# Moving the last subtraction of layer 1's softplus from VectorE to GpSimd

## The chip, the cores and the metric

One core of one Trainium2 chip. The metric is the device time of one execution in microseconds, the median over runs. The engines are named as in the profile: PE (TensorE; PEld is its weight load), DVE (VectorE), ACT (ScalarE), POOL (GpSimd), SP (SyncE, which issues most DMAs).

## The reference, cut to what matters

Three blocks follow one another over 2 x 576 = 1152 tokens with 512 features: an attention with a learned bias, a dense block (layer 1 and layer 2), and a routed block with one of 8 experts per token. The change lies in the dense block:

```python
def _moe_ref(x, w_in, w_out):                # x 1152 x 512, w_in 512 x 2048, w_out 2048 x 512
    h = x @ w_in                                             # layer 1
    g = np.maximum(h, 0.0) + np.log1p(np.exp(-np.abs(h)))    # softplus
    return (g @ w_out).astype(np.float32)                    # layer 2
```

## The kernel before, in words

The kernel runs in stages: attention (to about 175 us), layer 1 (175 to 277), layer 2 for the first six token tiles (to about 342), then layer 2 for the last three token tiles mixed with the routing, and the experts.

*Layer 1.* The 2048 hidden features are cut into 16 slices f of 128 (the loop at L627). The attention output lies transposed in SBUF, split into a high and a low part (x0hi, x0lo), and each weight slice likewise (whi, wlo). For a slice PE makes 3 x 12 matmuls at L640: three groups of 384 tokens, four chunks of 128 input features, and three products (high with high, high with low, low with high). The result ph takes three PSUM banks; two ph buffers take turns, so the matmuls of slice f+2 need that everything that reads ph of slice f is done.

*Softplus of a slice.* ACT computes ea = |h| (L653), ea = exp(-ea) (L654), la = ln(1 + ea) (L655) and ua = ea + 1 (L656), each over 128x1152. DVE then computes gA = max(h, 0) + la for the first 768 tokens (L657) and gB for the last 384 (L659); these two and L653 are the readers of ph. The rounding error that lies in 1 + ea is taken out afterwards: ua = (ua - 1) - ea (L661), then gA = gA - ua (L663) and gB = gB - ua (L664). Tiles ua, la and ea have two buffers each. gA and gB keep all 16 slices: gA is what layer 2 reads for token tiles 0 to 5, gB for the last three token tiles (it lies in the tiles gBt).

*Beside it on DVE and ACT.* The weights come as 64-bit floats and are converted and split on chip: L128 on ACT, L129, L130, L131 and L133 on DVE, then L149 (ACT) and L150 (DVE) for the slices of w_in, L619 (ACT) and L620 (DVE) for those of w_out. During layer 1 this is done for the w_in slices ahead and for the first four w_out slices.

*Layer 2.* g is split into a high and a low part again: L681 on ACT and L682 on DVE, from gA and, for the last three token tiles, from gB; the matmuls are L673 to L675.

*Order.* In the attention stage the order on each engine is the order written (a manual schedule). There GpSimd has work beside DVE: L316 scales the softmax rows, while DVE makes, among others, the hidden values of the bias (L219). In layers 1 and 2 no order is written by hand: the compiler's scheduler orders the instructions of each engine from dependences, the order of the program and its own costs, and sets the semaphores. In layer 1 no instruction runs on GpSimd; later ones are memsets and the indirect DMAs of the experts.

Of the kernel before, what the change touches and what calls it, by code (L numbers as in the profile page):

```python
# [17 lines left out]
ALU = mybir.AluOpType  # L18
# [59 lines left out]
def build(ctx: ExitStack, tc: tile.TileContext, I, out, dbg=None):  # L78
    nc = tc.nc
# [56 lines left out]
    def win_tiles(pool, f):  # L136
        return tuple(pool.tile([P, 4, P], F32R, tag=k, name=f"{k}{f}", bufs=NW1) for k in ("whi", "wlo"))
# [14 lines left out]
    def win_load(pool, f, whi, wlo):  # L152
        yield from win_split(pool, f, win_raw(pool, f), whi, wlo)

    def run(gen):
        for _ in gen:
            pass
# [4 lines left out]
    with ExitStack() as ac:  # L162
# [261 lines left out]
        with tc.manual_schedule(engines=order | {nc.sync.engine}):  # L424
# [60 lines left out]
            for n in range(N + DEPTH + 2):  # L485
# [13 lines left out]
                if n == 8:  # L499
                    nc.vector.tensor_reduce(out=sel4, in_=ident.rearrange("p (c e) -> p e c", c=4), axis=AX.X,  # L500
                                            op=ALU.add)
# [89 lines left out]
    with ExitStack() as mc:  # L591
# [20 lines left out]
        gB = [gBt[0][:, f] if f < 4 else gBt[1][:, f - 4] for f in range(16)]  # L612

        def wout_load(f):
            raw = wp2.tile([P, DM, 2], U32, tag="raw", name=f"raw_out{f}")
            nc.sync.dma_start(raw.rearrange("p f w -> p (f w)"), I["moe_w_out"].bitcast(U32)[P * f:P * f + P, :])
            w32 = wp2.tile([P, DM], F32, tag="w32", name=f"wout{f}", bufs=1)
            run(f64_to_f32(wp2, raw, w32, f"cout{f}"))
            nc.scalar.copy(wohi[f], w32)  # L619
            nc.vector.tensor_tensor(out=wolo[f], in0=w32, in1=wohi[f].bitcast(F32), op=ALU.subtract)  # L620

        with ExitStack() as c1:
            c1.push(x0c)
            c1.push(wc)
            sp = c1.enter_context(tc.tile_pool(name="sp", bufs=2, side="right", reuse_waits="tile"))
            ps_h = c1.enter_context(tc.tile_pool(name="ps_h", bufs=2, space=PSUM, reuse_waits="tile"))
            for f in range(16):  # L627
                if f >= 16 - 2 * NW0 and f % 2 == 0:
                    wout_load((f - 16 + 2 * NW0) // 2)
                whi, wlo = win_ready.pop(0)  # L630
                if f + NW1 < 16:
                    win_ready.append(win_tiles(wp, f + NW1))
                    run(win_load(wp, f + NW1, *win_ready[-1]))
                ph = ps_h.tile([P, 3, 512], F32, tag="ph", name=f"ph{f}")
                for n in range(3):
                    xk, o = (0, 384 * n) if n < 2 else (1, 0)
                    k = 0
                    for c in range(4):
                        for ws, xs in ((whi, x0hi), (whi, x0lo), (wlo, x0hi)):
                            nc.tensor.matmul(ph[:, n, :384], ws[:, c, :], xs[xk][:, c, o:o + 384],  # L640
                                             start=(k == 0), stop=(k == 11))
                            k += 1
                if f == 14:
                    for k, (ghi, glo) in enumerate(g0):
                        g = gA[k].rearrange("p a n -> p (a n)")[:, :2 * P]
                        nc.scalar.copy(ghi, g)
                        nc.vector.tensor_tensor(out=glo, in0=g, in1=ghi.bitcast(F32), op=ALU.subtract)
                hv = ph[:, :, :384]
                ua = sp.tile([P, 3, 384], F32, tag="ua", name=f"ua{f}")
                la = sp.tile([P, 3, 384], F32, tag="la", name=f"la{f}")  # L650
                ea = sp.tile([P, 3, 384], F32, tag="ea", name=f"ea{f}")

                nc.scalar.activation(ea, hv, AF.Abs)  # L653
                nc.scalar.activation(ea, ea, AF.Exp, scale=-1.0)  # L654
                nc.scalar.activation(la, ea, AF.Ln, bias=1.0)  # L655
                nc.scalar.activation(ua, ea, AF.Copy, bias=1.0)  # L656
                nc.vector.scalar_tensor_tensor(out=gA[f], in0=hv[:, 0:2], scalar=0.0, in1=la[:, 0:2],  # L657
                                               op0=ALU.max, op1=ALU.add)
                nc.vector.scalar_tensor_tensor(out=gB[f], in0=hv[:, 2], scalar=0.0, in1=la[:, 2],  # L659
                                               op0=ALU.max, op1=ALU.add)  # L660
                nc.vector.scalar_tensor_tensor(out=ua, in0=ua, scalar=1.0, in1=ea,  # L661
                                               op0=ALU.subtract, op1=ALU.subtract)
                nc.vector.tensor_tensor(out=gA[f], in0=gA[f], in1=ua[:, 0:2], op=ALU.subtract)  # L663
                nc.vector.tensor_tensor(out=gB[f], in0=gB[f], in1=ua[:, 2], op=ALU.subtract)  # L664


        c2 = ExitStack()
# [589 lines left out]
```

## Time and profile before

| what | us |
|---|---|
| median of 3 runs | 439.5 (438.65 to 441.52) |
| the profiled execution | 438.52 |
| its span, first to last instruction | 436.7 |

The profile is of one execution. In rows of instructions the first number is the start in us from the span's start, the second the duration in us, then engine, line, operation, output and inputs, shapes and count; in square brackets stands how long the engine sat idle before and what ended that. DVE starts an instruction shortly before the one ahead has ended, so durations in a row overlap a little. PEclk is the granted TensorE clock as a share of 2.4 GHz.

### The profile page before, as it was taken

To read this page: it belongs to the slowest core of one execution; us is meant where nothing else is said; L and a number is where in the kernel's file an instruction comes from. 1 tells how busy PE (TensorE), PEld (TensorE's weight loads), DVE (VectorE), ACT (ScalarE), POOL (GpSimd) and SP (SyncE) were. 2 spreads that over 40 slices of the span, in tenths; PEclk is the share of its full clock that TensorE was granted. 3 is DMA by queue.
4 is the path that set the end of the run, shared out by engine and by line. 5 is a ranking of instruction groups with operands and counts; after the bars stand their busy time and mean duration, and the time that the engine had idled before them with its cause. 6 is when DMAs were issued, how large, how long until landed. Compare 5 with 4: busy or idle time off the path is not lost.

```text
span 436.7 us, 8984 instructions
## 1 busy us (share of the span) xinstructions
PE 416.5 (95%) x3355; PEld 325.6 (75%) x3355; DVE 334.0 (76%) x869; ACT 276.5 (63%) x520; POOL 71.1 (16%) x97
## 2 busy tenths in 40 slices
PE   8989999999999998999999999999999998999994
PEld 6225667676677666999999999878888776877741
DVE  5799788889989877799999999999993425625501
ACT  5788888888899896698987878844551332121010
POOL 3014342333455541000000000000000000201001
PEclk9999999999999999999999999999999999999998
DMA  6799974766874413431323101133430700799600
GB/s 167 208 267 374 350 247 139 223 176 175 228 244 171 173 50 114 169 105 49 103 91 95 50 2 48 23 124 96 146 97 0 288 2 2 262 366 404 252 2 23
DMA packets 38579, 66.60 MB, mean 153 GB/s; under 512 B 4288, under 2 KB 17860, under 8 KB 38528
## 3 DMA queue, kind: packets, MB, share of 16 engines
q1 hardware_dynamic: 37520, 64.38, 45.9%
q10 hardware_dynamic: 592, 0.80, 0.5%
q0 software_dynamic: 416, 0.77, 0.5%
q8 instruction: 28, 0.46, 0.4%
q14 instruction: 23, 0.19, 0.1%
HBM read 49.80 MB, written 16.69 MB: 152 GB/s over the span
## 4 chain that ended last, share of the span: by engine, by line
PE 57%; DVE 10%; ACT 4%; issue 1%; DMA 1%; POOL 0%; POOLq 0%; DVEq 0%; ACTq 0%
PE ph L640 17%; PE px L673 5%; PE px L674 5%; PE px L675 5%; PE po L369 4%; PE sc L297 2%; PE bhA L980 2%; PE bhB L980 2%; PE byB L988 2%; PE pt L327 1%; DMA xbJ<-out_dram,tiJ 1%; DVE hid L219 1%; DVE ua L661 1%; PE sc_None L297 1%; DVE ep L303 1%
## 5 line engine op out<-in xcount | busy, mean ns | idle before, releaser
L316 POOL TENSOR_SCALAR ep<-ep,st 128x576 f32<-128x576 f32 x62 | 51.7, 846 | 93.5 <-DVE st L314 64.1
L640 PE MATMUL ph<-x0hi,whi 128*128 128x384 f32 x192 | 64.5, 336 | 0.6 <-DVE gBt L659 0.6
L640 PE MATMUL ph<-x0hi,wlo 128*128 128x384 f32 x192 | 64.2, 334 | 0.0
L640 PE MATMUL ph<-x0lo,whi 128*128 128x384 f32 x192 | 64.2, 334 | 0.0
L219 DVE TENSOR_SCALAR hid<-U 128x320 f32<-128x320 f32 (+17 forms) x134 | 56.4, 480 | 2.4 <-PE pb L224 2.3
L297 PE MATMUL sc<-kst,qr 64*128 64x288 f32 x256 | 50.9, 431 | 2.3 <-DVE st L303 1.9
L309 ACT ACTIVATE ep<-ep,st 128x576 f32<-128x576 f32 x64 | 49.0, 772 | 0.0
L297 PEld LDWEIGHTS sc<-kst,qr 64*128 64x128 f32 x256 | 28.8, 185 | 25.5 <-issue 12.5
L303 DVE CUSTOM_DVE_ANT_0 ep<-sc,bias 128x576 f32<-128x576 f32 x64 | 45.6, 750 | 2.8 <-PE sc L297 1.7
L232 ACT ACTIVATE bsb<-pb,isc 128x287 f32<-128x287 f32 (+31 forms) x72 | 31.7, 493 | 17.1 <-PE pb L224 15.8
L224 PE MATMUL pb<-hid,pw 128*32 128x512 f32 (+18 forms) x320 | 37.7, 486 | 2.0 <-ACT bsb L232 1.9
L369 PE MATMUL po<-at,vn 128*64 128x128 f32 (+1 forms) x512 | 38.4, 292 | 0.3 <-DVE x0lo L387 0.3
L640 PEld LDWEIGHTS ph<-x0hi,whi 128*128 128x128 f32 x192 | 36.0, 188 | 1.9 <-issue 1.6
L640 PEld LDWEIGHTS ph<-x0lo,whi 128*128 128x128 f32 x192 | 36.0, 188 | 0.0
L640 PEld LDWEIGHTS ph<-x0hi,wlo 128*128 128x128 f32 x192 | 36.0, 188 | 0.0
L347 ACT COPY at<-pt 128x512 f32<-128x512 f32 x64 | 34.1, 586 | 1.8 <-PE sc L327 0.7
L369 PEld LDWEIGHTS po<-at,vn 128*64 128x64 f32 x512 | 29.1, 136 | 4.2 <-DVE x0lo L387 0.5
L327 PEld LDWEIGHTS pt<-ident,ep 64*128 64x128 f32 x512 | 26.9, 138 | 5.5 <-issue 1.2
L327 PE MATMUL pt<-ident,ep 64*128 64x64 f32 x512 | 29.6, 226 | 0.9 <-ACT at L347 0.9
L681 ACT CAST ghiB<-gBt 128x384 fp32r<-128x384 f32 x16 | 8.2, 513 | 29.6 <-PE px L674 29.6
L682 DVE TENSOR_TENSOR gloB<-gBt,ghiB 128x384 fp32r<-128x384 f32 x16 | 8.9, 556 | 21.2 <-ACT ghiB L681 16.0
L673 PE MATMUL px<-wohi,ghiA 128*128 128x512 f32 x64 | 25.0, 390 | 0.0
(416 smaller groups left out, 860.7 us busy)
## 6 DMA issues: line engine op xcount, KB each, us to landing
biasd<-bsb SPq DMA_DIRECT2D x40, 295.5 KB, 3.6
bias<-biasd SPq DMA_DIRECT2D x19, 576.0 KB, 5.4
raw_in<-in_moe_w_in_dram SPq DMA_DIRECT2D x16, 512.0 KB, 3.8
raw_out<-in_moe_w_out_dram SPq DMA_DIRECT2D x16, 512.0 KB, 3.4
ex<-in_moe_w_dram SPq DMA_DIRECT2D x8, 1024.0 KB, 15.5
ew<-in_moe_w_dram SPq DMA_DIRECT2D x4, 1024.0 KB, 4.8
qr<-in_p_q_dram SPq DMA_DIRECT2D x10, 256.0 KB, 4.8
kst<-in_p_k_dram SPq DMA_DIRECT2D x8, 288.0 KB, 6.7
```

Of the source, the lines that this page charges most:

```text
L219: nc.vector.tensor_scalar(self.hid[c][:, :self.R], U[:, :self.R], Lt[:, g:g + 1], 0.0, ALU.add, ALU.max)
L224: nc.tensor.matmul(ps[32 * c:32 * c + 32, :hi - lo], w2b, self.hid[c][:, lo:hi], start=True, stop=True, tile_position=(0, 32 * c))
L232: nc.scalar.mul(dst, src, isc[:, s:s + 1])
L297: nc.tensor.matmul(self.sc[j][qs_, c, :288], self.q[js, self.hp, b, qs_], kst[js, self.hp, b, 288 * c:288 * c + 288], start=True, stop=Tru ...
L303: nc.vector.tensor_tensor_reduce(out=self.ep[:, j].rearrange("p (c k) -> p c k", c=2), in0=self.sc[j][:, :, :288], in1=bias.rearrange("p ( ...
L309: nc.scalar.activation(self.ep[:, j], self.ep[:, j], AF.Exp, bias=self.st[:, j, 0:1], scale=-1.0, accum_out=self.st[:, j, 1:2])
L316: eng.tensor_scalar(self.ep[:, j], self.ep[:, j], self.st[:, j, 3:4], 0.0, ALU.mult, ALU.add)
L327: nc.tensor.matmul(self.pt[:, r, c] if c < 8 else p5[r], flat[rs_, o:o + P], ident[rs_, rs_], is_transpose=True, start=True, stop=True, ti ...
L347: nc.scalar.copy(at.rearrange("p j c n -> p (j c) n")[:, :, off:off + 64], self.pt[:, r])
L369: nc.tensor.matmul(po[64 * j:64 * j + 64, :n], vn[:, self.hp, c, self.b, j, :], at[:, j, c, :n], start=(c == 0), stop=False, tile_position ...
L640: nc.tensor.matmul(ph[:, n, :384], ws[:, c, :], xs[xk][:, c, o:o + 384], start=(k == 0), stop=(k == 11))
L673: nc.tensor.matmul(px, ghi[:, cs], wohi[f], start=(f == 0), stop=False)
```

## The change

The subtraction at L664, one per slice and 16 in all, is issued on GpSimd instead of VectorE. Operands, tiles and all other lines stay.

```diff
                 nc.vector.tensor_tensor(out=gA[f], in0=gA[f], in1=ua[:, 0:2], op=ALU.subtract)
-                nc.vector.tensor_tensor(out=gB[f], in0=gB[f], in1=ua[:, 2], op=ALU.subtract)
+                nc.gpsimd.tensor_tensor(out=gB[f], in0=gB[f], in1=ua[:, 2], op=ALU.subtract)
```

## Rows read from the trace of the kernel before

**Rows 1.** The page's first part: busy time and share of the span.

```profile
PE 416.5 (95%) x3355; PEld 325.6 (75%) x3355; DVE 334.0 (76%) x869; ACT 276.5 (63%) x520; POOL 71.1 (16%) x97
```

**Rows 2.** Busy time of each engine in layer 1.

```profile
core 0: us, PE busy (x) PEld busy (x) DVE busy (x) ACT busy (x) POOL busy (x), PEclk, DMA share, GB/s
174.70:276.80 102.10, 101.45 (x583) 100.47 (x582) 98.43 (x154) 86.39 (x100) 0.00 (x0) 1.00 0.24 76
```

**Rows 3.** PE's waits, 174.7 to 342: us in total, times, longest.

```profile
PE ph L640 <- DVE gBt L659: 0.6, 1, 0.6
PE px0pl L675 <- DVE gloA L682: 0.3, 1, 0.3
```

**Rows 4.** PE in order of time: first matmuls of blocks and of layer 2.

```profile
174.71 0.44 PE L640 MATMUL ph<-x0hi,whi 128*128 128x384 f32 x1
...
187.30 0.36 PE L640 MATMUL ph<-x0hi,whi 128*128 128x384 f32 x1
...
206.32 0.33 PE L640 MATMUL ph<-x0hi,whi 128*128 128x384 f32 x1
...
212.56 0.35 PE L640 MATMUL ph<-x0hi,whi 128*128 128x384 f32 x1
...
251.74 0.41 PE L640 MATMUL ph<-x0hi,whi 128*128 128x384 f32 x1 [0.65 <-DVE gBt L659]
...
276.78 0.39 PE L675 MATMUL px0pl<-wohi,glo 128*128 128x512 f32 x1
```

**Rows 5.** DVE in order of time, slice 0 of layer 1.

```profile
186.56 0.55 DVE L659 SCALAR_TENSOR_TENSOR gBt<-ph,la 128x384 f32<-128x384 f32 x1
187.02 1.35 DVE L661 SCALAR_TENSOR_TENSOR ua<-ua,ea 128x1152 f32<-128x1152 f32 x1
188.29 0.68 DVE L150 TENSOR_TENSOR wlo<-win,whi 128x512 fp32r<-128x512 f32 x1
...
189.76 0.55 DVE L664 TENSOR_TENSOR gBt<-gBt,ua 128x384 f32<-128x384 f32 x1
190.23 0.68 DVE L133 SCALAR_TENSOR_TENSOR win<-raw_in,cin6a 128x512 uint32<-128x512 uint32 x1
```

**Rows 6.** The tile gBt: durations in ns (min/median/max), first and last start.

```profile
L664 DVE TENSOR_TENSOR gBt<-gBt,ua x16: 549/552/554, 189.8 to 285.3; 128x384 f32<-128x384 f32 x16
L681 ACT CAST ghiB<-gBt x16: 512/513/515, 329.9 to 376.5; 128x384 fp32r<-128x384 f32 x16
```

**Rows 7.** POOL's groups by line: busy us, mean ns, idle before.

```profile
L316 POOL TENSOR_SCALAR ep<-ep,st 128x576 f32<-128x576 f32 x62 | 51.7, 846 | 93.5 <-DVE st L314 64.1 <-DVE x0lo L387 12.9 <-ACT at L347 6.8
...
L190 POOL MEMSET v<- 128x1024 f32 x1 | 0.9, 941 | 0.0
L921 POOL MEMSET xbB<- 128x512 f32 x1 | 0.5, 545 | 0.0
```

**Rows 8.** DVE beside POOL in order of time, around 125 and 141 us.

```profile
124.93 1.12 DVE L133 SCALAR_TENSOR_TENSOR win<-raw_in,cin0a 128x512 uint32<-128x512 uint32 x1
...
124.76 0.75 POOL L316 TENSOR_SCALAR ep<-ep,st 128x576 f32<-128x576 f32 x1 [1.41 <-ACT x0hi L383]
...
140.99 0.69 DVE L150 TENSOR_TENSOR wlo<-win,whi 128x512 fp32r<-128x512 f32 x1
...
141.14 1.17 POOL L316 TENSOR_SCALAR ep_None<-ep_None,st_None 128x576 f32<-128x576 f32 x1 [1.48 <-ACT whi L149]
```

**Rows 9.** DVE, then POOL, in order of time around 108 us.

```profile
107.67 0.50 DVE L219 TENSOR_SCALAR hid<-U 128x560 f32<-128x560 f32 x1
...
108.51 0.92 DVE L219 TENSOR_SCALAR hid<-U 128x560 f32<-128x560 f32 x1
109.35 0.99 DVE L219 TENSOR_SCALAR hid<-U 128x560 f32<-128x560 f32 x1
...
107.76 1.36 POOL L316 TENSOR_SCALAR ep<-ep,st 128x576 f32<-128x576 f32 x1 [2.79 <-DVE x0lo L387]
109.10 0.93 POOL L316 TENSOR_SCALAR ep<-ep,st 128x576 f32<-128x576 f32 x1
```

## The prediction

> **What bounds the kernel now.** I read the page first, then the table of the two stretches around the change, then who waited for whom, then the instructions in order of time. The page shows TensorE (PE) busy for 95% of the 436.7 us span and VectorE (DVE) for 76% [rows 1]. That share hides the stage that matters. In layer 1 (174.7 to 276.8 us) DVE is busy 98.4 us of 102.1 while GpSimd (POOL) is not busy at all, and the TensorE clock is granted at its upper level (1.00, 2.4 GHz) [rows 2]. The reader is to see two engines loaded to the brim beside an idle one.
>
> Which of the two sets the pace? The list of waits names only one wait of PE on DVE in layer 1, 0.6 us, and one of 0.3 us early in layer 2 [rows 3]. The starts of the blocks say a little more. An undisturbed slice f of layer 1 (36 matmuls) takes from 206.32 to 212.56, that is 6.24 us; 16 of them are 99.8 us. Layer 1 takes from 174.71 to 276.78, that is 102.1 us [rows 4]. So some 2.2 us go to PE standing still or starting late, 0.65 of it the labelled wait at 251.74 [rows 4]. The reason is the pair of ph buffers: slice f+2 can't start before L657 and L659 of slice f have read theirs. L659 of slice 0 ends at 186.56 + 0.55 = 187.11 and PE starts slice 2 at 187.30, 0.19 us later [rows 4, 5]. PE is thus the bound, with DVE about a tenth of a microsecond behind it: DVE work taken away can give back 2.2 us of layer 1 at most, DVE work added comes out as time almost at once.
>
> **The change part by part.**
>
> *Removed from DVE:* 16 subtractions L664 of 128x384, 552 ns each [rows 6]. DVE overlaps the end of one instruction with the start of the next, so the place in the queue that one gives back is start to start: 189.76 to 190.23, 0.47 us [rows 5]. 16 x 0.47 = 7.5 us of DVE, all inside layer 1 but the last two slices, whose L659 PE doesn't wait for in layer 1; 14 x 0.47 = 6.6 us bear on PE.
>
> *Added to GpSimd:* 16 subtractions with two inputs from SBUF. The trace has none. Nearest rows: two memsets, 128x1024 in 941 ns and 128x512 in 545, so 0.77 ns per element and 0.15 us fixed; and the tensor_scalar of 128x576, 846 ns in the mean [rows 7], 0.75 us where nothing delays it [rows 8]. (0.75 - 0.15) / 576 = 1.04 ns per element read. If two inputs are streamed side by side, 384 x 1.04 + 0.15 = 0.55 us; if one after the other, 768 x 1.04 + 0.15 = 0.95 us; if the fixed part and a slower loop both come on top, twice the whole tensor_scalar, 1.5 us. I take 0.95, the one between. POOL is idle in layer 1 [rows 2], so the 16 never queue behind one another at a period of 6.2 us, and no DMA is issued behind them there; the memset of a later stage is all that follows.
>
> *Nobody is late for the result itself:* gB is first read by the cast L681 at 329.9, 44 us after the last L664 at 285.3 [rows 6]. The ua buffer (two deep) is now released by POOL, and is written again by L656 two slices, about 12 us, later; POOL's finish about 1.6 us (one DVE instruction of delay and 0.95) after L661 is far inside that. The rooms of layer 1's tiles that layer 2 takes over are released by the last POOL instruction instead of the last L664, at most about 1 us later; that bounds a cost from above, and I take nothing, because PE's only wait early in layer 2 is one of 0.3 us for something else [rows 3], taken up below.
>
> *What does cost: DVE and POOL delay each other.* The attention stage shows it. Four equal DVE instructions L219 follow one another; the first starts at 107.67 and lasts 0.50, the third and fourth start at 108.51 and 109.35 and last 0.92 and 0.99 [rows 9]. The two that lengthen stand beside the two POOL instructions that start at 107.76 and 109.10. POOL's first takes 1.36 us instead of 0.75: it waits for DVE, then DVE waits for it. Together DVE loses 0.42 + 0.49 = 0.91 us to 2 x 0.75 = 1.5 us of POOL work. An instruction with two inputs suffers too: L133 takes 1.12 us beside a POOL instruction [rows 8] and 0.68 alone [rows 5], a loss of 0.44. And POOL waits behind a two-input DVE instruction, 1.17 us behind L150 [rows 8]. So one POOL instruction of 0.75 us costs DVE about 0.45 us, 0.30 less than its own time, or six tenths of it.
>
> In layer 1 POOL's subtraction becomes ready when L661 ends. DVE then has the next instruction, a split of weights or L663, started without a gap (L150 at 188.29 in slice 0 [rows 5]); POOL gets in behind it and the DVE instruction after that waits. With 0.95 us the loss is 0.57 (six tenths) to 0.65 (0.30 less); I take 0.60. DVE's balance per slice is -0.47 + 0.60 = +0.13 us, and over 14 slices +1.8 us. Some of it falls into the 3.7 us that DVE still idles in layer 1 [rows 2], mostly in the first slices, and a POOL instruction that meets L657 or L659 may cost nothing; I leave 0.8 off and keep +1.0 us. The balance is small because the change swaps a DVE instruction for a wait of DVE of about the same length.
>
> The Trainium skill, "GPSIMD Engine Reference", section "3. Performance versus the Vector engine", puts a two-input elementwise instruction on GpSimd at 1.96 times VectorE's time. On L664 that would be an estimate of 1.08 us, a loss of about 0.7 and some +3 us over the 14 slices; no run here shows the ratio.
>
> *After layer 1* PE's only wait on DVE, 0.3 us [rows 3], is for a gloA; even if all of it went, 0.3 us would be won, and I count none; the rest of the kernel shifts with the end of layer 1.
>
> *Sum.* The profiled execution took 438.5 us (span 436.7 and 1.8 around it). 438.5 + 1.0 = 439.5 in its terms. The median of the runs shown is 439.5, 1.0 above this execution, so the forecast in the median's terms is **440.5 us**: no change that can be told (about 1%, 4.4 us, is what a measurement of this kernel can tell from none).
>
> **The rivals.**
>
> *A. DVE wins.* If POOL streams both inputs together (0.55 us) the loss is 0.25 to 0.33 and DVE's balance -0.14 to -0.22 per slice; if POOL mostly meets L657 and L659, it is the full -0.47. PE's 2.2 us of late starts [rows 4] then shrink, half to all of them: 439.5 - 2.2 = 437.3 at best, some 438.3 in the middle. For it: POOL is idle, and 0.13 us per slice is little to be wrong by. Against it: POOL becomes ready in the middle of DVE's two-input work, not beside L657. Faster by over 1% isn't in it, since layer 1 has only 2.2 us to give.
>
> *B. The exchange makes DVE the bound of layer 1 (slower).* Its place is the DVE instruction behind POOL's in every slice; its price is POOL's whole time instead of six tenths. With 0.95 us blocked in full DVE's balance is +0.48 per slice, 14 x 0.48 = 6.7 us, 446.2; with 0.55 it is +0.08, or 1.1 us. It decides from a loss of 0.47 us up: beyond that every tenth of a microsecond is 1.4 us of kernel. For it: DVE idles only 3.7 us of 102 [rows 2] and PE starts within 0.2 us of the release [rows 4, 5]. Against it: the four rows of L219 show a loss smaller than POOL's time [rows 9]. The Trainium skill, "SBUF — State Buffer", section "Who interferes with whom", speaks for this one: a VectorE instruction with two SBUF inputs and a GpSimd instruction that reads SBUF exclude each other, and the second blocks in full until the first is done. That L133 and L150's neighbour both stretch agrees with the exclusion [rows 8]; that the loss is only six tenths doesn't agree with a price of the whole time.
>
> *C. Another order.* Outside the attention stage the compiler's scheduler orders each engine's instructions from its own costs; with 16 fewer on DVE it may pull weight splits ahead of L657 or behind it. The shown order already costs 2.2 us, so the swing is of that size: 437.5 to 442.5.
>
> **How the numbers follow.** Forecast 0.48 (own range 439 to 442), A 0.22, B 0.18, C 0.12. The range that leaves two in ten out goes from A's best, 437.3, to the middle of B, 444.5. Faster by over 1%: below 435.1, only an order of C much better than the present one, 0.03. Slower by over 1%: above 443.9, two thirds of B and a little of C, 0.14. Same: 0.83.
>
> **What would show it.** In the profile after: L664 on POOL x16 near 0.95 us without a wait and up to 1.5 with one; DVE instructions that follow L661 lengthened by about 0.6 us, L657 and L659 not; DVE's busy time in layer 1 about as before although 8.8 us of instructions left it; layer 1 between 102 and 104 us. A step is wrong if the L664 on POOL lasts over 1.2 us (then B), if DVE rows stay at their old lengths (then A), or if layer 1 is longer with DVE idle in it (then C). The forecast fails if layer 1 changes by more than 4 us.

## The result and the profile after

| | before | after |
|---|---|---|
| median of 4 runs each, us | 439.07 (438.30 to 441.52) | 444.06 (442.85 to 445.45) |
| ratio of after to before | | 1.009, 95% interval 1.0061 to 1.0120 |
| the profiled execution and its span, us | 438.52, 436.7 | 442.85, 441.1 |

The change makes the kernel slower, by 5.0 us in the medians and 4.3 in the two profiled executions. The page of after, first part and the new group of POOL (busy us, mean ns, idle before); it answers to [rows 1, 6]:

```profile
PE 417.5 (95%) x3355; PEld 325.7 (74%) x3355; DVE 336.1 (76%) x853; ACT 277.6 (63%) x520; POOL 105.9 (24%) x113
...
L664 POOL TENSOR_TENSOR gBt<-gBt,ua 128x384 f32<-128x384 f32 x16 | 35.0, 2189 | 87.7 <-DVE ua L661 65.8
```

DVE has 16 instructions fewer and is busy 2 us longer. POOL's subtractions take 2.19 us in the mean, their waiting included, where 0.95 was forecast. The stretch of layer 1 in after, which answers to [rows 2], and PE's waits (us in total, times, longest), which answer to [rows 3]:

```profile
174.64:280.47 105.83, 102.74 (x582) 100.43 (x581) 101.62 (x145) 88.14 (x101) 31.83 (x14) 1.00 0.25 79
```

```profile
PE ph L640 <- DVE gBt L659: 1.1, 3, 0.5
PE px0pl L675 <- DVE gloA L682: 1.0, 1, 1.0
PE ph L640 <- ACT whi L149: 1.0, 2, 0.6
PE ph L640 <- ACT ea L653: 1.0, 1, 1.0
```

Layer 1, from its first matmul to the first of layer 2, takes 105.83 us instead of 102.07, that is 3.76 more; the wait for gloA early in layer 2 grows from 0.3 to 1.0 us. Together they are the span's 4.4 us within a tenth: the time was lost in layer 1 and in this one wait behind it.

What happens there is plain in the order of time. DVE and POOL of after in two slices; of slice 1 only the instructions from L150 to L659 of the next slice:

```profile
188.23 0.69 DVE L150 TENSOR_TENSOR wlo<-win,whi 128x512 fp32r<-128x512 f32 x1
188.45 1.34 POOL L664 TENSOR_TENSOR gBt<-gBt,ua 128x384 f32<-128x384 f32 x1 [21.93 <-issue]
188.83 1.77 DVE L663 TENSOR_TENSOR gA<-gA,ua 128x768 f32<-128x768 f32 x1
...
195.67 0.68 DVE L150 TENSOR_TENSOR wlo<-win,whi 128x512 fp32r<-128x512 f32 x1
195.82 4.15 POOL L664 TENSOR_TENSOR gBt<-gBt,ua 128x384 f32<-128x384 f32 x1 [6.04 <-DVE ua L661]
196.27 0.95 DVE L663 TENSOR_TENSOR gA<-gA,ua 128x768 f32<-128x768 f32 x1
...
198.68 0.41 DVE L130 TENSOR_SCALAR cin8a<-cin8m 128x512 uint32<-128x512 uint32 x1
199.01 0.95 DVE L657 SCALAR_TENSOR_TENSOR gA<-ph,la 128x768 f32<-128x768 f32 x1
199.88 0.54 DVE L659 SCALAR_TENSOR_TENSOR gBt<-ph,la 128x384 f32<-128x384 f32 x1
```

In slice 0 POOL waits for L150, then runs, and L663 waits for POOL: 1.77 us instead of 0.95. In slice 1 POOL starts about as soon after L150's start (0.15 us, 0.22 in slice 0), but DVE keeps the turn: L663 and four more follow undisturbed, and POOL ends only at 199.97, after DVE has come to L657. L657 and L659 are not lengthened. The tile ua over all slices of after (ns: min/median/max), and the three lengthened DVE instructions that are not L663:

```profile
L663 DVE TENSOR_TENSOR gA<-gA,ua x16: 946/1768/1779, 188.8 to 287.4; 128x768 f32<-128x768 f32 x16
L664 POOL TENSOR_TENSOR gBt<-gBt,ua x16: 1132/1416/4414, 188.4 to 287.5; 128x384 f32<-128x384 f32 x16
```

```profile
236.82 0.85 DVE L129 TENSOR_SCALAR cin13m<-cin13m 128x512 f32<-128x512 f32 x1 [0.31 <-ACT cin13m L128]
...
264.37 1.40 DVE L131 SCALAR_TENSOR_TENSOR cout4a<-raw_out,cout4a 128x512 uint32<-128x512 uint32 x1
...
288.30 1.51 DVE L620 TENSOR_TENSOR wolo<-wout,wohi 128x512 fp32r<-128x512 f32 x1
```

L663 is lengthened by 0.82 us in nine slices, 7.4 us in all; with these three (0.43, 0.72, 0.83) DVE loses 9.4 us in 12 slices. In the other four (1, 3, 4 and 6) it loses nothing. That is against the 7.5 us that it was relieved of. Two of the twelve blocks, those of the last two slices (L663 at 281.21 and L620 at 288.30), lie behind layer 1; inside it ten blocks take 7.7 us, against 14 subtractions or 6.6 us of relief. L129 reads a single input: an instruction with one input can be blocked too.

But the scheduler also gave DVE, ACT and PE another order of instructions. So two theories stood. Theory 1: DVE and POOL exclude each other, and the blocks cost the time. Theory 2: the new order costs it.

### The profile page after: what moved, and what is told of

Same layout as the page of the kernel before. It is cut to its first block, busy times and chain, and to the rows that moved or that the text cites. A ratio compares the mean times of both kernels' runs of the same rounds, so it can differ in the third digit from the quotient of the medians.

```text
span 441.1 us, 8989 instructions
## 1 busy us (share of the span) xinstructions
PE 417.5 (95%) x3355; PEld 325.7 (74%) x3355; DVE 336.1 (76%) x853; ACT 277.6 (63%) x520; POOL 105.9 (24%) x113
## 4 chain that ended last, share of the span: by engine, by line
PE 56%; DVE 10%; ACT 5%; issue 2%; DMA 1%; POOL 0%; POOLq 0%; DVEq 0%; ACTq 0%
PE ph L640 13%; PE px L673 6%; PE px L674 6%; PE px L675 6%; PE po L369 4%; PE sc L297 2%; PE bhA L980 2%; PE bhB L980 2%; PE byB L988 2%; DVE gA L663 2%; PE pt L327 1%; DMA xbJ<-out_dram,tiJ 1%; DVE gA L657 1%; DVE hid L219 1%; PE sc_None L297 1%
## 5 line engine op out<-in xcount | busy, mean ns | idle before, releaser
L219 DVE TENSOR_SCALAR hid<-U 128x320 f32<-128x320 f32 (+17 forms) x134 | 56.4, 480 | 2.4 <-PE pb L224 2.3
L664 POOL TENSOR_TENSOR gBt<-gBt,ua 128x384 f32<-128x384 f32 x16 | 35.0, 2189 | 87.7 <-DVE ua L661 65.8
L682 DVE TENSOR_TENSOR gloB<-gBt,ghiB 128x384 fp32r<-128x384 f32 x16 | 8.9, 557 | 21.9 <-ACT ghiB L681 16.8
```

The lines of the kernel that those rows point to most:

```text
L219: nc.vector.tensor_scalar(self.hid[c][:, :self.R], U[:, :self.R], Lt[:, g:g + 1], 0.0, ALU.add, ALU.max)
L664: nc.gpsimd.tensor_tensor(out=gB[f], in0=gB[f], in1=ua[:, 2], op=ALU.subtract)
```

## The experiments

Each kernel differs from before or after by the lines shown. In all but e3 and e8 the order of instructions on PE, DVE, ACT and SP is exactly that of after; in e3 it is that of before. In e8 it is after's but for the one subtraction that goes back to DVE and, from about 302 us on, well inside layer 2, some weight work and casts of DVE and ACT that changed places. e1 to e4 were measured beside a median of 439.77 us for before, e5 to e8 beside 440.86; the ratios are not exactly the quotients of the medians. In the profiled executions layer 1 starts anywhere from 173.76 to 175.89 us, though no edit touches what lies ahead of it, so what a block costs is read from layer 1 itself.

**e1: no subtraction, after's order.**

```diff
-                nc.gpsimd.tensor_tensor(out=gB[f], in0=gB[f], in1=ua[:, 2], op=ALU.subtract)
+                pass
```

> The subtraction L664 is left out on every engine (gB keeps the rounding error of 1 + ea); the order of the instructions on PE, DVE, ACT and SP is that of the changed kernel, instruction for instruction. Theory 1 (DVE and POOL exclude each other): no POOL instruction, so L663 takes 0.95 us in all 16 slices, DVE is 7.5 us lighter than before, and the time is at most 2.2 us under that of before: 437 to 438.5 us. Theory 2 (the new order costs the time): still slower than before, 441 to 444 us.

Measured: 439.13 us beside 439.77 for the kernel before on the same chip, ratio 0.9978 (0.9951 to 1.0005). Layer 1 in e1:

```profile
174.34:275.60 101.26, 101.25 (x583) 100.61 (x582) 94.55 (x145) 87.68 (x101) 0.00 (x0) 1.00 0.25 81
```

Theory 2 falls: with after's order and no POOL instruction layer 1 is the shortest yet, 0.8 us under before. The medians don't tell e1 from before, and e1's lies 0.6 us above the range expected. The row holds a second lesson: of the 6.6 us that left layer 1 with 14 subtractions, some 2.6 were filled by five weight instructions that the new order brings forward into it, 0.8 shortened it, and the rest is idle time of DVE: 101.26 - 94.55 = 6.7 us, where it was 3.7. Most of the new idle time is this wait in layer 1 of e1 (0.2 us before), and both its places are late in layer 1, at 266.89 and 273.13:

```profile
DVE gA L657 <- ACT la L655: 3.4, 2, 2.3
```

There DVE is early and waits for ACT's logarithm. PE gets 0.8 us of the 6.6, and it has no more to get: the list of waits names none of PE's in layer 1 of e1.

**e2: POOL only writes.**

```diff
+                nc.gpsimd.memset(ua[:, 2], 0.0)
```

(in place of the subtraction.)

> In place of L664 POOL sets a third of ua to zero after L661: it writes SBUF, reads none, and releases ua; the subtraction for gB is left out. Order on the other engines as in the changed kernel. Theory 1 with exclusion only of reads: as e1_none within 0.7 us, L663 at 0.95 us in all slices. Theory 1b (any POOL instruction blocks DVE): L663 lengthened by about 0.4 us, 439 to 443 us. Theory 2: as the changed kernel, 441 to 444 us.

Measured: 440.12 us, ratio 1.0007 (0.9983 to 1.0032). Tile ua and layer 1 in e2:

```profile
L664 POOL MEMSET ua<- x16: 418/422/638, 189.3 to 283.7; 128x384 f32 x16
L663 DVE TENSOR_TENSOR gA<-gA,ua x16: 950/952/959, 189.7 to 283.6; 128x768 f32<-128x768 f32 x16
```

```profile
175.56:276.83 101.27, 101.26 (x582) 100.62 (x581) 94.56 (x145) 87.65 (x101) 6.75 (x14) 1.00 0.25 82
```

Layer 1 is that of e1 to a hundredth. POOL's memset, which reads no SBUF, costs DVE nothing, and the release of ua by POOL costs nothing either. The median is 1.0 us above e1's where 0.7 was allowed; the two profiled executions differ by 1.2 us at the start of layer 1 (175.56 and 174.34), ahead of everything that differs between the kernels.

**e3: the same POOL load on top of before, in before's order.**

```diff
                 nc.vector.tensor_tensor(out=gB[f], in0=gB[f], in1=ua[:, 2], op=ALU.subtract)
+                nc.gpsimd.tensor_tensor(out=scr, in0=gA[f][:, 0], in1=ua[:, 2], op=ALU.subtract)
```

> L664 stays on DVE as before, and POOL makes a subtraction of the same size with two inputs into a spare tile after it; nothing reads that. The order on PE, DVE, ACT and SP is that of the kernel before. Theory 1: no relief, and the block of 0.8 us in some ten slices on top: layer 1 longer by 6 to 9 us, 445 to 449 us, in the old order. Theory 2: as the kernel before within 1 us.

Measured: 447.89 us over five executions (444.81 to 448.95; a sixth took 453.30 and isn't counted), ratio 1.0218 (1.0169 to 1.0267). Theory 1 holds in the old order too. The profiled execution is the fastest: layer 1 takes 104.70 us (+2.6 on before, where 6 to 9 were expected) and PE waits 2.6 us in layer 2, soon behind it:

```profile
PE px0pl L673 <- ACT ghiA L681: 2.6, 1, 2.6
PE ph L640 <- DVE gBt L659: 1.8, 5, 0.8
```

Here L663 keeps its 0.95 us; POOL comes later in the slice and hits L129, L130, L131, L150, L647 and L682 instead, eight instructions in all. One of them is L129 with its single input, 0.42 us long when nothing is beside it:

```profile
241.43 1.21 POOL L664 TENSOR_TENSOR scr<-gA,ua 128x384 f32<-128x384 f32 x1 [4.14 <-DVE gA L663]
241.67 1.25 DVE L129 TENSOR_SCALAR cin13m<-cin13m 128x512 f32<-128x512 f32 x1
```

The slower executions were not profiled, so how the blocks fell in them stays open.

**e4: the same subtraction on POOL, at a better time.**

```diff
-                nc.scalar.activation(la, ea, AF.Ln, bias=1.0)
+                cue = nc.scalar.activation(la, ea, AF.Ln, bias=1.0)
...
+                late = (f and late(cue.ins.name), lambda c, g=gB[f], u=ua: tc.add_manual_dep(nc.gpsimd.tensor_tensor(out=g, in0=g, in1=u[:, 2], op=ALU.subtract).ins, c, mybir.DependencyInfo(mybir.DependencyClass.Sync, mybir.DependencyReason.DATA), reason="late"))[1]
+            late(cue.ins.name)
```

> The changed kernel, but POOL's subtraction for slice f also waits for la of slice f+1 (L655), that is for the time when DVE comes to L657 and L659, which read PSUM and only one input from SBUF. Orders on all engines as in the changed kernel; one wait more on POOL. Theory 1: POOL's 0.9 us fall beside L657 and L659 (1.33 us) in most slices, L663 stays at 0.95 us, 437 to 439 us. Theory 2: 442 to 445 us.

Measured: 439.31 us over eleven executions (a twelfth took 444.20 and isn't counted), 0.3 above the range expected; ratio 1.0013 (0.9982 to 1.0044). Layer 1 of e4, one of its slices in order of time, and PE's wait behind layer 1:

```profile
173.76:274.98 101.22, 101.22 (x583) 100.57 (x582) 94.52 (x145) 87.70 (x101) 15.59 (x14) 1.00 0.26 82
```

```profile
197.33 0.96 DVE L657 SCALAR_TENSOR_TENSOR gA<-ph,la 128x768 f32<-128x768 f32 x1
197.38 1.02 POOL L664 TENSOR_TENSOR gBt<-gBt,ua 128x384 f32<-128x384 f32 x1 [5.03 <-ACT la L655]
198.21 0.55 DVE L659 SCALAR_TENSOR_TENSOR gBt<-ph,la 128x384 f32<-128x384 f32 x1
```

```profile
PE px0pl L675 <- DVE gloA L682: 0.9, 1, 0.9
```

One wait more for each of POOL's instructions gives back the 4.6 us of layer 1 that the change loses against e1. POOL's instruction now takes 1.02 us, beside L657 and L659 at their old lengths. No DVE instruction in layer 1 of e4 is lengthened. What it is worth against the kernel before can't be told from none.

**e5: the same wait at the wrong time.** As e4, but the cue is L653, |h|:

```diff
-                nc.scalar.activation(ea, hv, AF.Abs)
+                cue = nc.scalar.activation(ea, hv, AF.Abs)
```

> As e4_late, one wait more on POOL's subtraction for slice f, but for |h| of slice f+1 (L653) instead of its la (L655): POOL then comes two ACT instructions, some 2.5 us, earlier, in the middle of DVE's two-input work. Orders on all engines as in the changed kernel. Theory 1 (what counts is which DVE instruction runs beside POOL): DVE instructions between L661 and L657 are lengthened by about 0.8 us in most slices, layer 1 at 103.5 to 106.5 us, 441.5 to 445 us. Rival (a later or a waiting POOL instruction is enough): as e4_late, layer 1 at 101.2 us, 438 to 440 us.

Measured: 445.51 us, ratio 1.0113 (1.0073 to 1.0152). Layer 1 and the tile ua in e5:

```profile
175.32:281.87 106.55, 103.18 (x583) 100.26 (x582) 101.54 (x145) 88.25 (x101) 29.03 (x14) 1.00 0.24 77
```

```profile
L663 DVE TENSOR_TENSOR gA<-gA,ua x16: 941/950/1774, 189.5 to 288.8; 128x768 f32<-128x768 f32 x16
```

As slow as after, slightly past the ranges that were expected. Fewer L663 are hit, and L129, L131, L133, L620 and L682 in their place. It is the DVE instruction beside POOL that counts, not the wait.

**e6 and e7: smaller prices.** Half the columns, and one input instead of two:

```diff
+                nc.gpsimd.tensor_tensor(out=gB[f][:, :192], in0=gB[f][:, :192], in1=ua[:, 2, :192], op=ALU.subtract)
```

```diff
+                nc.gpsimd.tensor_copy(ea[:, 2], ua[:, 2])
```

> The changed kernel with POOL's subtraction over 192 of the 384 columns (the other half of the correction for gB is left out). Orders as in the changed kernel. Theory 1 with a price that is POOL's own time: the lengthening falls from 0.82 to 0.4 to 0.5 us, layer 1 at 101.5 to 103.5 us, 439.5 to 441.5 us. If the price is fixed per instruction: L663 lengthened by 0.8 as in the changed kernel, 443 to 445 us.

> The changed kernel with a copy of 128x384 from ua to ea on POOL in place of the subtraction, so one input read instead of two (the correction for gB is left out). Orders as in the changed kernel. If any read of SBUF by POOL excludes DVE's two-input instructions: they are lengthened by POOL's shorter time, 0.3 to 0.5 us, layer 1 at 101.5 to 103.5 us, 439.5 to 441.5 us. If it takes two inputs on both sides: no lengthening, layer 1 at 101.3 us as in e1_none and e2_writeonly.

Measured: e6 441.82 us, 0.3 above its range, ratio 1.0033 (0.9997 to 1.0068); e7 441.18 us, ratio 1.0007 (0.9978 to 1.0036). The medians are too close to before to tell; the profiles aren't. L663 and layer 1, first e6, then e7:

```profile
L663 DVE TENSOR_TENSOR gA<-gA,ua x16: 943/1350/1366, 189.7 to 285.3; 128x768 f32<-128x768 f32 x16
...
175.50:278.48 102.98, 102.23 (x582) 100.54 (x581) 97.54 (x145) 87.97 (x101) 26.01 (x14) 1.00 0.25 81
```

```profile
L663 DVE TENSOR_TENSOR gA<-gA,ua x16: 941/1254/1261, 190.1 to 285.4; 128x768 f32<-128x768 f32 x16
...
175.89:278.51 102.62, 102.09 (x583) 100.48 (x582) 96.85 (x145) 88.02 (x101) 22.41 (x14) 1.00 0.25 81
```

A block takes 0.82 us for 384 columns of two inputs, 0.40 for 192 columns of two, 0.30 for 384 columns of one. The price is thus not fixed per instruction: it is 2.1 ns per column with two inputs and 0.8 with one, and one input suffices. In one and the same order layer 1 is thus 101.26 us without a block (e1), 102.62 with 0.30 (e7), 102.98 with 0.40 (e6) and 105.83 with 0.82 (after).

**e8: e4 with the last slice back on DVE.** In e4 the last POOL subtraction ran beside L620 (1.50 us).

```diff
-            late(cue.ins.name)
+            nc.vector.tensor_tensor(out=gB[f], in0=gB[f], in1=ua[:, 2], op=ALU.subtract)
```

> As e4_late, but the subtraction of the last slice stays on DVE: in e4_late POOL's last one ran beside L620, which took 0.82 us more, and PE waited 0.9 us for gloA after layer 1. Theory 1: layer 1 stays at 101.2 us, the wait for gloA falls to 0.3 us or less, 0.6 us less than e4_late: 438 to 439 us, 0.5 to 1.5 us under the kernel before. Rival (that wait has another cause): wait and time as e4_late.

Measured: 439.91 us beside 440.86 for before, so 0.9 less, as expected, though above the 438 to 439 named; ratio 0.9980 (0.9953 to 1.0007). Layer 1 takes 101.27 us and PE's wait behind it is

```profile
PE px0pl L675 <- DVE gloA L682: 0.4, 1, 0.4
```

Half a microsecond of the 0.9 went, as the theory has it, though not down to 0.3; the subtraction itself is back on DVE ahead of gloA. No version that was run is faster than before beyond its interval; e8's upper end misses by less than a tenth of a per cent (e1's too, but e1 leaves the subtraction out).

## Why the prediction was right or wrong

*The verdict "no change that can be told", 440.5 us:* the ratio is 1.009 and its interval excludes 1, so a slowdown can be told, though it is under the 1% that the prediction set as its mark. 444.06 lies in the outer range (to 444.5) and outside the forecast's own (439 to 442). That the forecast's sign held is luck: the sum behind it doesn't carry it, as the balance below shows. What came is rival B. Three of the prediction's signs said so: L664 on POOL lasts over 1.2 us in all but two slices, the blocked DVE instructions grow by 0.82 and not 0.6, and layer 1 lies outside 102 to 104 us.

*The ceiling of a gain, 2.2 us in layer 1:* right as a bound, but too high. With all 16 subtractions gone (e1) layer 1 gains 0.8 us. The prediction put all 2.2 down to the ph buffers; in e1 PE has no listed wait in layer 1, and it still takes 1.4 us more than 16 x 6.24. What these 1.4 us are stays open.

*POOL's own time, 0.95 us:* near; it takes 1.02 us when nothing stands in its way (e4). The ratio to VectorE in the Trainium skill, "GPSIMD Engine Reference", section "3. Performance versus the Vector engine", 1.96 at 2048 columns, gave an estimate of 1.08; measured here at 384, 1.02 to 0.55 is 1.86.

*DVE's loss per POOL instruction, 0.60 us:* too small as a price, near as a mean. It measured 0.82 where POOL gets in, but only ten of the 14 slices of layer 1 lost anything, so that the mean over them is 7.7 / 14 = 0.55 us; that price and count nearly cancel is luck. The six tenths came from L219 and L133 beside tensor_scalar instructions with one input [rows 8, 9]. Their 0.45 us over 576 columns is 0.8 ns per column, just what e7's copy with one input costs (0.30 over 384); with two inputs it is 2.1 (after and e6). So the rows held the right price for one input, and as a share of POOL's time it was carried over to an instruction with two. That a slice can lose nothing the forecast had allowed for only as a small discount.

*The balance, -0.47 + 0.60 per slice:* this is the step that failed. Relief and loss were set against each other one for one, and the runs show that they weigh differently. Over the 14 slices that the forecast's +1.8 us was for, blocks and relief net +7.7 - 6.6 = +1.1 us, by luck about what the forecast kept (+1.0), yet layer 1 grew by 3.8. In one order, e1 to after, 7.7 us of blocks cost 4.6 us; the relief of 6.6, together with the new order, was worth 0.8, since PE then has no listed wait left in layer 1, and DVE fills part of the room with weight work and waits for ACT's la in the rest (3.4 us in e1).

*Rival B:* right in its place and its kind of price. Its threshold of 0.47 is too high: against before (102.07) layer 1 is longer by 0.5 us with blocks of 0.30 (e7) and by 0.9 with 0.40 (e6), since the relief is worth so little. Its sum with 0.82 would be 14 x 0.35 = 4.9 us; the medians moved by 5.0, but this closeness is partly chance, as only ten of those 14 slices lost, and the relief counted for less than B set. The Trainium skill, "SBUF — State Buffer", section "Who interferes with whom", was the better guide than the discounted price: VectorE instructions with two SBUF inputs and GpSimd instructions that read SBUF exclude each other, and VectorE instructions in a 2-port mode and GpSimd's do too. It agrees with e2 (no read, no block), with e4 (L657 and L659 unhurt, one input in PSUM) and with 0.82 of 1.02 us blocked. L129 and L219, with one input, are lengthened as well; no run here shows in which mode they run.

*Rival A:* POOL did meet L657 in four slices, but only after it had lost the turn. *Rival C:* the order did change, and e1 shows that by itself it costs nothing in layer 1.

*"Costs nothing" for the release of the rooms:* right as such (e2), but the last subtraction cost 0.7 us by the wait for gloA, through L620 beside it, a place that the working didn't look at.

## What to carry to other kernels

Moving work from DVE to an idle GpSimd can be no relief while DVE runs instructions that read all their inputs from SBUF: a POOL instruction that reads SBUF then blocked them for most of its length here, two-input ones and L129 and L130 with one alike, 0.82 us for 0.47 us saved. If it must move, set it beside DVE work that reads PSUM, by a wait on whatever starts that work; here one such wait gave back all that layer 1 had lost. And a relief is worth only what the next engine in the chain lets through, here 0.8 us of 6.6, so it can't be netted against a loss.

## What was not expected of the hardware

POOL doesn't get its turn in the order of asking. In after it starts 0.15 us into L150 both at 195.82, where DVE runs five more instructions ahead of it (4.15 us in all), and at 201.76, where it gets in behind L150 and L663 takes 1.77 us:

```profile
201.62 0.69 DVE L150 TENSOR_TENSOR wlo<-win,whi 128x512 fp32r<-128x512 f32 x1
201.76 1.42 POOL L664 TENSOR_TENSOR gBt<-gBt,ua 128x384 f32<-128x384 f32 x1 [1.80 <-DVE ua L661]
202.23 1.77 DVE L663 TENSOR_TENSOR gA<-gA,ua 128x768 f32<-128x768 f32 x1
```

Four of 16 subtractions went the first way, with up to 4.41 us; what decides was not tried.
